# The last two units' input projections made together, with seven products of halves

## The chip, the cores and the metric

One Trainium2 chip, one of its cores. The metric is the device time of one execution of the kernel in microseconds (us): the median of several runs.

## The reference

A linear attention with a decaying state (RWKV-6) is followed by a feed-forward block. All data is fp32.

```python
# r, k, v, w: (4 batches, 8 heads, 768 tokens, 48);  u: (8, 48)
for t in range(S):
    cur = u * k_t (outer) v_t
    y[t] = r_t @ (state + cur)
    state = w_t * state + k_t (outer) v_t
x = y as (3072 tokens, 384)
h = x @ w_in                    # w_in: (384, 2048)
g = h * erf(softplus(h))
out = g @ w_out                 # w_out: (2048, 384)
```

## The kernel before

**Units.** The work is cut into 12 units (n_steps), numbered 0 to 11. A unit has 128 tokens of each of two batches, so 256 tokens (UNIT). A unit goes through three parts: its attention step, which leaves xTs[s], the unit's tokens transposed (384 inner dimensions as KT = 3 blocks of 128 partitions, by 256 tokens); its input projection (hidden); its output projection (project, or project_fast from unit 3 on). The three parts of neighbouring units are interleaved: while step s runs its attention, TensorE is given pieces of the input projection of unit s-1 and of the output projection of unit s-3.

**Input projection.** The 2048 hidden dimensions are 16 blocks of 128, in two groups of FG = 8 (g = 0 and 1). hidden makes two blocks per piece: six products of 128x128 weights by 128x256 tokens (L1027) into one PSUM tile m, of which there are two; ScalarE copies it into the SBUF tile h (L1036). Two pieces make one chunk of 128x1024.

**Activation.** For each chunk ScalarE does softplus into room[:, 0] (softplus_chunk, L983) and erf into the PSUM of y or of pp1 (erf_chunk, L987), and VectorE multiplies h by it in place (multiply_chunk, L992). Softplus and erf need different function tables, so a table load stands before each.

**Output projection.** project_fast does the product of h and w_out as seven products of halves instead of eight. blend makes sums and differences of quarters of h on VectorE (L1112 to L1118, four instructions of 128x1024); mix_weights did the same for w_out once. It yields seven times; each of the seven pieces is eight products of 192 columns (L1135), with copies and adds into o (L1141 to L1167) and the output's DMA.

**Order.** It is written out by hand. From step 5 on, attend_late runs a step and calls run at seven places ("front", "near", 0 to 4); each place has a string of tokens in LATE or USUAL, which run_late executes in order: s, e and m are softplus, erf and multiplication of the next chunk; H is a piece of the input projection of unit s-1; P a piece of the output projection of unit s-3; S the blend of unit s-2; k and F other helpers. After the last step the strings stand in the code: the rest of the attention of unit 11 (from_own L584, fence L593, through_state L610, with the six DMAs of L645 that complete xTs[11]), then

```python
run_late(s, "s P")                      # s = 12, between the two from_own
run_late(s, "m ey m P s P P ep m P P P S H H s H ey m H H s H ep m H H")
run_late(s + 1, "s P ey m P s P P ep m P P P S")
run_late(s + 2, "P P P P P P P")
```

Each engine's instructions stay in the order in which they are emitted, and engines wait for each other through semaphores.

**Names in what follows.** level_products (L552) and take_level work out the attention within a block; state_part (L659) and the adds into middle (L736) carry the state to the second half of the tokens; kT (L718) is an operand of state_part; scale is L328. pp0 and pp1 are two PSUM tiles (products), y another, of the same size, and m two of half that size. words, rest, in, w, rk1, h and o are rotating SBUF tiles.

Of the kernel before, what the change touches and what calls it, by code (L numbers as in the profile page):

```python
# [11 lines left out]
FP32 = mybir.dt.float32  # L12
I32 = mybir.dt.int32
U32 = mybir.dt.uint32
AF = mybir.ActivationFunctionType
ALU = mybir.AluOpType

P = 128
# [5 lines left out]
FG = 8  # L24
FT = 2
# [36 lines left out]
def kernel(  # L62
# [14 lines left out]
    nc = tc.nc  # L77
    PSUM = bass.MemoryType.PSUM

    n_steps, _, _, JP, C = rkw.shape  # L80
    NH, D = v.shape[2:]
    NP = JP // NJ
    NE = NH // JP
    NB, n_pairs = out.shape[:2]
    _, NT, DM = w_out.shape
    KT = DM // P
    UNIT = NJ * C
    NG = NT // FG
# [5 lines left out]
    ins = ctx.enter_context(tc.tile_pool(name="ins", bufs=2))  # L94
    att = ctx.enter_context(tc.tile_pool(name="att", bufs=2))
    xs = ctx.enter_context(tc.tile_pool(name="xs", bufs=2))
    hid = ctx.enter_context(tc.tile_pool(name="hid", bufs=4))
# [33 lines left out]
    def products(shape, n=None):  # L131


        if n is not None:
            return ps_p.tile(shape, FP32, name=f"pp{n}")
        n = turns["next"]
        turns["next"] = 1 - n
        return ps_p.tile(shape, FP32, name=f"pp{n}")
# [934 lines left out]
    def mix_weights():  # L1073

        upper, lower = w_out_sb[:, :FG], w_out_sb[:, FG:]
        b11, b12, b21, b22 = (x[:, :, k * ND : (k + 1) * ND] for x in (upper, lower) for k in range(2))
        t3, t2, t4 = (mixed[:, n] for n in range(3))
        for of, a, op, b in (
            (t3, b22, ALU.subtract, b12), (t2, t3, ALU.add, b11),
            (t4, b21, ALU.subtract, t2), (b12, b12, ALU.subtract, b11),  # L1080
        ):
            engine = yield
            engine.tensor_tensor(out=of, in0=a, in1=b, op=op)
        yield

    blends, lanes = {}, {}

    def quarter(of, what):
# [8 lines left out]
    def blend(of, *parts):  # L1097

        if of not in blends:
            if of < n_steps - 1:  # L1100
                tiles = [room[:, n] for n in (1, 2, 3)]
            else:
                two = att.tile([P, 2, JP, C], FP32, name="rk1", bufs=1)
                one = ins.tile([P, JP, C], FP32, name="w")
                tiles = [x.rearrange("p n t -> p (n t)") for x in (two[:, 0], two[:, 1], one[:])]
            s1, s2, s4 = (x.rearrange("p (f t) -> p f t", t=C) for x in tiles)
            blends[of] = s1, s2, quarter(of, "21"), s4
        s1, s2, s3, s4 = blends[of]
        a = {what: quarter(of, what) if what not in lanes else lanes[what] for what in ("11", "12", "22")}
        for part in parts or (1, 2, 4, 3):  # L1110
            if part == 1:
                nc.vector.tensor_add(s1, s3, a["22"])  # L1112
            elif part == 2:
                nc.vector.tensor_sub(s2, s1, a["11"])
            elif part == 3:
                nc.vector.tensor_sub(s3, a["11"], s3)
            else:
                nc.vector.tensor_sub(s4, a["12"], s2)  # L1118

    def project_fast(s, gs):  # L1120
# [47 lines left out]
                nc.sync.dma_start(out=out[i * NJ, c, :, part], in_=o[0][:, part])  # L1168
        yield

    xTs, hids, projs = {}, {}, {}
    gated = [[] for _ in range(n_steps)]

# [18 lines left out]
    def piece(kind, of):  # L1192
        if not 0 <= of < n_steps:
            return
        if of not in kind:
            if kind is hids:
                kind[of] = hidden(of, xTs[of], gated[of], not of)
            else:
                kind[of] = (project_fast if of >= FAST else project)(of, gated[of])
        next(kind[of])  # L1200

    def in_order(s, k):
# [3 lines left out]
        for what in order[k]:  # L1206
# [12 lines left out]
            "S2 S3 H k12y S4 H F", "s H ep m H H F G s H H H ep",  # L1219
        ),  # L1220
        n_steps - 1: (
            "s P", "m", "ey P m s P P ep P", "m P P", "S", "H H", "s H ey m H H s H ep H H"
        ),
    }
    USUAL = (
# [4 lines left out]
    def run_late(s, tokens, following=None):  # L1230

        for what in tokens.split():
            if what == "A":
                advance()
            elif what == "P":
                piece(projs, s - 3)
            elif what == "H":
                piece(hids, s - 1)
            elif what == "F":
                next(following, None)  # L1240
            elif what == "G":
                mixing.send(nc.gpsimd)
            elif what == "s":
                softplus_chunk()
            elif what[0] == "e":
                erf_chunk(what[1])
            elif what == "m":
                multiply_chunk()
            elif what[0] == "k":
                to_lane(s - 2, what[1:3], what[3])  # L1250
            else:
                blend(s - 2, *(int(n) for n in what[1:]))
                if what == "S3":
                    del lanes["11"], lanes["22"]
                elif what == "S4":
                    del lanes["12"]
# [10 lines left out]
    }  # L1267
    ALONE = {1, 2}

    mixing = mix_weights()  # L1270
    next(mixing)
    make_identity(nc, ident[:])
# [10 lines left out]
    with tc.manual_schedule(  # L1283
        engines={getattr(mybir.EngineType, x) for x in ("PE", "DVE", "Activation", "Pool", "SP")}
    ):
        stay_warm(6)
        for t in (*states[0], *states[1], middle):
            nc.gpsimd.memset(t[:], 0.0)
        nc.gpsimd.memset(over_blocks[:], 1.0)
        nc.scalar.copy(u_row[:, :1], ident[:, :1])  # L1290
        stages, send = convert(
            [
                (into[:, f : f + 2, :], given[:, f : f + 2, :])
                for into, given in ((w_in_sb, w_in), (w_out_sb, w_out))
                for f in range(0, NT, 2)
            ]
        )
        stages["l"](0, loaded[0][0][:, 1, JP - 1, C - 1 : C])
        for s in range(n_steps):
            xTs[s] = xs.tile([P, KT, UNIT], FP32, name="xT")  # L1300
            places = iter(range(8))

            def convert_at(n, late=True):
                if s < len(CONVERT) and n < len(CONVERT[s]):
                    send(CONVERT[s][n][late])

            def place(n):
                if n == LOG - 1 and DIRECT - 1 <= s <= DIRECT:
                    load_rows(s + 2)
                for due in {(3, 4): (5,), (4, 3): (6,), (4, 5): (7,)}.get((s, n), ()):  # L1310
                    load_w(due)
                if s >= DIRECT:
                    in_order(s, next(places))
                    return
                if s in ALONE:
                    if s == 2 and not n:

                        next(hids[0])
                        turns.pop("ahead")()
                    convert_at(n)  # L1320
                    if (s, n) == (1, LOG - 1):
                        load_w(3)
                        load_v(2)
                    if (s, n) == (2, LOG - 2):
                        load_v(3)
                        nc.sync.dma_start(out=block_sb[:], in_=block_mask)
                        nc.sync.dma_start(out=u_row[:], in_=u_rows)
                    if s == 2 and not n:
                        beside(s, next(places))
                        advance(STAGES[s][n])  # L1330
                        return
                    advance(STAGES[s][n])
                else:
                    advance(STAGES[s][n])
                    convert_at(n)
                    if s == DIRECT - 1 and not n:
                        load_rows(DIRECT)
                beside(s, next(places))

            def run(n, following):  # L1340
                if n == 3 and s < n_steps - 2:
                    load_rows(s + 2)
                if n == 3 and s + 3 < n_steps:
                    load_w(s + 3)
                run_late(s, LATE.get(s, USUAL)[STAGES_LATE.index(n)], following)

            if s > DIRECT:
                attend_late(s, run)
                continue
            if s:  # L1350
                attend(
                    s, xTs[s], lambda n: convert_at(n, False), place, lambda: convert_at(LOG + 2)
                )
            else:
                attend_first(xTs[s])
            if s and s + 2 < n_steps:
                load_step(s + 2)
        s = n_steps
        from_own(s - 1, ready[s - 1][0], 1)
        fence()  # L1360
        run_late(s, "s P")
        from_own(s - 1, ready[s - 1][0], 0)
        through_state(s - 1, xTs[s - 1])
        run_late(s, "m ey m P s P P ep m P P P S H H s H ey m H H s H ep m H H")
        run_late(s + 1, "s P ey m P s P P ep m P P P S")
        run_late(s + 2, "P P P P P P P")


# [94 lines left out]
```

## Time and profile before

| | us |
|---|---|
| median of 3 runs | 588.79 |
| lowest and highest | 587.59, 589.34 |
| the profiled execution, its own time | 591.17 |
| its span, first to last instruction | 589.3 |
| TensorE busy | 582.3 (99%) |
| VectorE busy | 434.6 (74%) |
| ScalarE busy | 361.2 (61%) |
| GpSimd busy | 273.4 (46%) |

The span is the time between the first and last instruction of the profiled execution; what lies around it (1.9 us) is in the execution's own time. The mean granted TensorE clock was 0.994. Busy TensorE time is modelled at the ends of matmuls; the chain of waits, which follows the last instruction back to whatever released it, says better where the time goes. A page's row gives line, engine, operation, output and inputs, number, busy time, mean time of one, and the idle time before.

### The profile page before, as it was taken

How to read it: one execution, taken by the hardware profiler on the slowest of the kernel's cores; microseconds unless marked ns; L12 is line 12 of the kernel's file. 1: busy time of each engine (PE TensorE's matmuls, PEld its weight loads, DVE VectorE, ACT ScalarE, POOL GpSimd, SP SyncE). 2: the span in 40 equal slices, each digit the busy share in tenths (PEclk: the TensorE clock that was granted, in tenths of full speed). 3: DMA queues.
4: the chain of work that ended last, by engine and by line, in shares of the span. 5: the costliest groups of instructions: out<-in, count | busy, mean ns of one | idle time of the engine just before them, and what ended most of it. 6: DMA issues, size and time to landing. Idle time of an engine off the chain costs nothing.

```text
span 589.3 us, 16635 instructions
## 1 busy us (share of the span) xinstructions
PE 582.3 (99%) x7256; PEld 500.6 (85%) x7256; DVE 434.6 (74%) x523; ACT 361.2 (61%) x474; POOL 273.4 (46%) x313
## 2 busy tenths in 40 slices
PE   8899999999999999999999999999999999999997
PEld 6688887688668768998998998998898898898997
DVE  6775886899996899799799799799799525023140
ACT  3567878644544598756766766766766754746720
POOL 4557381702398479569369369369359000000000
PEclk9899999999999999999999999999999999999999
DMA  7577572440432514234334334333331300000000
GB/s 258 185 258 292 187 238 61 172 153 10 143 110 103 135 45 160 46 133 153 65 128 159 65 128 150 73 125 116 73 121 42 73 21 14 3 19 15 1 27 28
DMA packets 54081, 63.24 MB, mean 107 GB/s; under 512 B 35160, under 2 KB 40568, under 8 KB 52984
## 3 DMA queue, kind: packets, MB, share of 16 engines
q1 hardware_dynamic: 53624, 61.98, 33.2%
q8 instruction: 57, 0.93, 0.7%
q10 hardware_dynamic: 384, 0.20, 0.1%
q14 instruction: 16, 0.13, 0.1%
HBM read 52.39 MB, written 8.69 MB: 104 GB/s over the span
## 4 chain that ended last, share of the span: by engine, by line
PE 89%; DVE 8%; issue 1%; DMA 1%; POOL 0%; SPq 0%; DVEq 0%; POOLq 0%
PE m L1027 40%; PE m L1135 28%; PE m L1059 6%; PE pp L552 6%; PE y L584 2%; PE pp L659 2%; PE y L610 2%; DVE in L328 2%; PE m L862 1%; DVE words L467 1%; DVE rk L463 1%; DMA rest<-in_w_rows 1%; DVE sums L453 1%; PE pp L871 1%; DVE h L1016 1%
## 5 line engine op out<-in xcount | busy, mean ns | idle before, releaser
L1027 PE MATMUL m<-xT,w_in_sb 128*128 128x256 f32 x1152 | 256.8, 382 | 0.0
L1027 PEld LDWEIGHTS m<-xT,w_in_sb 128*128 128x128 f32 x1152 | 216.4, 190 | 30.5 <-ACT h L1036 0.3
L1036 ACT COPY h<-m 128x512 f32<-128x512 f32 x96 | 55.5, 578 | 83.1 <-PE m L1027 83.1
L328 DVE TENSOR_TENSOR in<-in,tot_sb 128x1024 f32<-128x1024 f32 (+1 forms) x55 | 74.6, 1357 | 15.9 <-PE pp L552 13.7
L463 POOL TENSOR_TENSOR rk<-words 128x528 f32<-128x528 f32 (+3 forms) x28 | 42.4, 1515 | 91.2 <-DVE sums L453 80.8
L467 POOL TENSOR_TENSOR words<-words,rest 128x528 f32<-128x528 f32 (+10 forms) x77 | 78.1, 1015 | 6.0
L1059 PE MATMUL m<-w_out_sb,h 128*128 128x384 f32 x192 | 64.3, 491 | 0.0
L1059 PEld LDWEIGHTS m<-w_out_sb,h 128*128 128x128 f32 x192 | 35.7, 190 | 23.5
L1135 PE MATMUL m<-mixed,h 128*128 128x192 f32 x288 | 51.1, 331 | 0.0
L983 ACT ACT_TABLE_LOAD x36 | 46.2, 1283 | 2.8 <-issue 2.1
L1135 PE MATMUL m<-w_out_sb,h 128*128 128x192 f32 x272 | 47.5, 329 | 0.0
L1135 PEld LDWEIGHTS m<-mixed,h 128*128 128x128 f32 x288 | 46.6, 190 | 0.9
L987 ACT ACT_TABLE_LOAD x36 | 46.2, 1283 | 1.6 <-DVE room L1118 1.1
L1135 PEld LDWEIGHTS m<-w_out_sb,h 128*128 128x128 f32 x272 | 44.3, 190 | 0.4
L1135 PE MATMUL m<-w_out_sb,room 128*128 128x192 f32 x256 | 44.2, 326 | 0.0
L552 PEld LDWEIGHTS pp<-in 48*64 48x64 f32 (+1 forms) x2368 | 33.4, 126 | 11.6 <-issue 6.0
L1135 PEld LDWEIGHTS m<-w_out_sb,room 128*128 128x128 f32 x256 | 42.0, 190 | 0.0
L992 DVE TENSOR_TENSOR h<-h,y 128x1024 f32<-128x1024 f32 x17 | 20.7, 1216 | 28.3 <-ACT y L987 28.1
L402 POOL TENSOR_TENSOR tot_sb<-tot_sb 128x256 f32<-128x256 f32 (+4 forms) x50 | 37.1, 742 | 3.8
L983 ACT ACTIVATE room<-h 128x1024 f32<-128x1024 f32 x36 | 38.1, 1057 | 0.4
L992 DVE TENSOR_TENSOR h<-h,pp 128x1024 f32<-128x1024 f32 x19 | 23.1, 1213 | 19.5 <-ACT pp L987 19.5
L552 PE MATMUL pp<-in 48*64 48x32 f32 (+1 forms) x2368 | 37.1, 212 | 0.2 <-DVE in L328 0.2
(147 smaller groups left out, 830.5 us busy)
## 6 DMA issues: line engine op xcount, KB each, us to landing
in<-in_rkw SPq DMA_DIRECT2D x8, 1024.0 KB, 5.7
words<-in_moe_w_in SPq DMA_DIRECT2D x16, 384.0 KB, 6.1
words<-in_moe_w_out SPq DMA_DIRECT2D x16, 384.0 KB, 5.8
words<-in_rk_rows SPq DMA_DIRECT2D x8, 768.0 KB, 6.4
w<-in_rkw SPq DMA_DIRECT2D x11, 512.0 KB
v<-in_v SPq DMA_DIRECT2D x12, 384.0 KB, 5.7
out<-o SPq DMA_DIRECT2D x23, 192.0 KB, 2.9
in<-in_rkw SPq DMA_DIRECT2D x7, 512.0 KB, 5.8
```

The source lines that it names most:

```text
L328: nc.vector.tensor_mul(halves, halves, view(tots[level - 1], 0, [[1, n], [2, nb], [0, half]]))
L402: nc.gpsimd.tensor_mul(new, pair[:, :, 0], pair[:, :, 1])
L463: engine.tensor_mul(terms[n], r[:, :, n:], k[:, :, : near - n])
L467: engine.tensor_mul(k[:, :, :m], k[:, :, :m], w[:, :, n : n + m])
L552: nc.tensor.matmul(to, lhsT=rk(1, n)[rows(e), s0 : s0 + m], rhs=right, start=True, stop=True,)
L983: nc.scalar.activation(sp_room, chunks[0], AF.Softplus)
L987: nc.scalar.activation(at, sp_room, AF.Erf)
L992: nc.vector.tensor_mul(h, h, at)
L1027: nc.tensor.matmul(ps[:, ff, :], lhsT=w_in_sb[:, g * FG + f + ff, kk * P : (kk + 1) * P], rhs=xT[:, kk, :], start=kk == 0, stop=kk == KT - 1,)
L1036: nc.scalar.copy(h[:, f : f + FT, :], ps[:])
L1059: nc.tensor.matmul(ps[j][:], lhsT=gs[g][:, f, j * C : (j + 1) * C], rhs=w_out_sb[:, g * FG + f, :], start=g + f == 0, stop=g == NG - 1 and ...
L1135: nc.tensor.matmul(to, lhsT=a[:, f], rhs=b[:, f], start=start and f == 0, stop=f == FG - 1, skip_group_check=True,)
```

## The change

The input projections of units 10 and 11 are no longer made one after the other, but together, at the very end. Written with the two groups of hidden blocks as rows, and the inner dimension's first two blocks of 128 as columns, w_in is a matrix of two by two; the tokens of the two units are the other factor, of two by two as well (inner block by unit). Seven products of such halves take the place of eight, with sums of weights (join_weights, s1 to s4, once) and differences of tokens (join_tokens, t1 to t4). The third inner block is added by plain products; where one plain product can serve two results, the difference of the two units' third blocks is used (less).

hidden_of_two yields seven times (J1 to J7 here) for each pair of blocks of both groups, four pairs in all. Its accumulators are m0, a half of y, low, a half of pp0, and high, a half of pp1; each holds 128x512. Results are copied by ScalarE or VectorE into h11, h21 (unit 10) and h12, h22 (unit 11), and later parts are added there by VectorE. The activation goes by chunks of 512 with new tokens: u is softplus, v is erf in place, z the multiplication. The last two chunks, of 1024, are done by s, e and m as before. The H, and the S, of the last step's places are taken out. Q is a P of one unit later; w one instruction of join_weights.

```diff
+    def half_room(name, shape):
+        t = wide.tile(shape, I32, name=name, bufs=3 if name == "words" else 2)
...
     def blend(of, *parts):
         if of not in blends:
-            if of < n_steps - 1:
+            if of < n_steps - 2:
                 tiles = [room[:, n] for n in (1, 2, 3)]
+            elif of == n_steps - 1:
+                tiles = [half_room("words", [P, 2, DM, 2])[:, : FG * C] for _ in range(3)]
             else:
                 two = att.tile([P, 2, JP, C], FP32, name="rk1", bufs=1)
...
+    def third(g, kk):
+        return w_in_sb[:, g * FG : (g + 1) * FG, kk * P : (kk + 1) * P]
+
+    def join_weights():
...
+        a11, a12, a21, a22 = (third(g, kk) for g in range(NG) for kk in range(2))
+        turns["joint weights"] = s1, s2, a21, s4
+        for out_, a, op, b in (
+            (s1, a21, ALU.add, a22), (s2, s1, ALU.subtract, a11),
+            (s4, a12, ALU.subtract, s2), (a21, a11, ALU.subtract, a21),
+        ):
+            nc.vector.tensor_tensor(out=out_, in0=a, in1=b, op=op)
+            yield
+
+    def join_tokens():
...
+        one, two = ([xTs[of][:, kk, :] for kk in range(KT)] for of in (n_steps - 2, n_steps - 1))
+        for out_, a, b in (
+            (t1, two[0], one[0]), (t2, two[1], t1), (t4, one[1], t2), (less, one[2], two[2]),
+            (t3, two[1], two[0]),
+        ):
+            nc.vector.tensor_sub(out_, a, b)
...
+    def hidden_of_two():
...
+        m0 = y[:, :, 0].rearrange("p e j t -> p e (j t)")
+        low, high = (products([P, NE, 2, UNIT], n)[:, :, 0] for n in range(2))
+        s1, s2, s3, s4 = turns["joint weights"]
+        x, z, t1, t2, t3, t4, less = turns["joint tokens"]
+        a11, a12, up, _, a22, down = (third(g, kk) for g in range(NG) for kk in range(KT))
+
+        def add_up(to, start, *factors):
+            for k, (a, b) in enumerate(factors):
+                for e in range(NE):
+                    nc.tensor.matmul(
+                        to[:, e], lhsT=a[:, 2 * i + e], rhs=b,
+                        start=start and not k, stop=True, skip_group_check=True,
+                    )
+
+        pairs = FG // 2
+        for i in range(pairs):
+            f = slice(2 * i, 2 * i + 2)
+            add_up(m0, True, (a11, x[0]))
+            nc.scalar.copy(h11[:, f], m0)
+            yield
+            add_up(low, True, (a12, x[1]), (up, x[2]))
+            nc.vector.tensor_add(h11[:, f], h11[:, f], low)
+            chunks.append(h11[:, f])
+            yield
+            add_up(high, True, (s1, t1))
+            nc.scalar.copy(h22[:, f], high)
+            yield
+            add_up(m0, False, (s2, t2))
+            nc.vector.tensor_copy(h12[:, f], m0)
+            yield
+            add_up(low, True, (a22, t4), (down, less))
+            nc.scalar.copy(h21[:, f], low)
+            yield
+            add_up(m0, False, (s3, t3), (down, z[2]))
+            nc.vector.tensor_add(h21[:, f], h21[:, f], m0)
+            nc.vector.tensor_add(h22[:, f], h22[:, f], m0)
+            chunks.append(h21[:, f])
...
+            yield
+            add_up(high, False, (s4, z[1]), (up, z[2]))
+            nc.vector.tensor_add(h12[:, f], h12[:, f], high)
...
+    def activate_pair(what):
+        if what == "u":
...
+            nc.scalar.activation(at, h, AF.Softplus)
...
+        elif what == "v":
+            h, at = slots["u"].pop(0)
+            nc.scalar.activation(at, at, AF.Erf)
...
+        else:
+            h, at = slots["v"].pop(0)
+            nc.vector.tensor_mul(h, h, at)
...
         n_steps - 1: (
-            "s P", "m", "ey P m s P P ep P", "m P P", "S", "H H", "s H ey m H H s H ep H H"
+            "s P", "m w", "ey P m s P P ep P", "m P P", "", "", ""
         ),
...
         s = n_steps
         from_own(s - 1, ready[s - 1][0], 1)
         fence()
-        run_late(s, "s P")
+        run_late(s - 1, "S Q w w w")
         from_own(s - 1, ready[s - 1][0], 0)
         through_state(s - 1, xTs[s - 1])
-        run_late(s, "m ey m P s P P ep m P P P S H H s H ey m H H s H ep m H H")
-        run_late(s + 1, "s P ey m P s P P ep m P P P S")
+        run_late(s, "P P P P T")
+        run_late(s, "J J J J J u J u u J")
+        run_late(s, "J u v J J v J z z J v v J z u u u J z")
+        run_late(s, "J u v J J v J z z J v v J z u u J z")
+        run_late(s, "J J u v J J z v J z v J z u v J z P P S s ey")
+        run_late(s + 1, "P P m s ep P P m P P P S")
         run_late(s + 2, "P P P P P P P")
```

T stands for join_tokens and the start of hidden_of_two, J for its next yield.

More of the change, by code (lines that the diff above doesn't have):

```diff
@@ L1084, in mix_weights @@
         yield
+    def half_room(name, shape):
+        t = wide.tile(shape, I32, name=name, bufs=3 if name == "words" else 2)
+        t = t[:].rearrange("p a b two -> p (a b two)" if len(shape) == 4 else "p a b -> p (a b)")
+        return t.bitcast(FP32)
     blends, lanes = {}, {}
@@ L1169, in project_fast @@
         yield
+    def third(g, kk):
+        return w_in_sb[:, g * FG : (g + 1) * FG, kk * P : (kk + 1) * P]
+    def join_weights():
+        s1, s2, s4 = (
+            half_room("words", [P, 2, DM, 2])[:, : FG * P].rearrange("p (f m) -> p f m", m=P)
+            for _ in range(3)
+        )
[7 more added lines that the diff above has]
+            yield
@@ new lines, in join_tokens @@
+    def join_tokens():
+        made = ins.tile([P, 2, JP, C], FP32, name="in")
+        made = made[:].rearrange("p x n t -> p (x n t)").rearrange("p (i t) -> p i t", t=UNIT)
+        t1, t2, t3, t4, less = (made[:, i] for i in range(5))
+        one, two = ([xTs[of][:, kk, :] for kk in range(KT)] for of in (n_steps - 2, n_steps - 1))
[4 more added lines that the diff above has]
+            nc.vector.tensor_sub(out_, a, b)
+        turns["joint tokens"] = one, two, t1, t2, t3, t4, less
@@ new lines, in hidden_of_two @@
+    def hidden_of_two():
+        one, two = n_steps - 2, n_steps - 1
+        h11, h21 = (hid.tile([P, FG, UNIT], FP32, name="h")[:] for _ in range(NG))
+        h12 = room[:, 2:4].rearrange("p i n -> p (i n)").rearrange("p (f t) -> p f t", t=UNIT)
+        h22 = ins.tile([P, 2, JP, C], FP32, name="in")
+        h22 = h22[:].rearrange("p x n t -> p (x n t)").rearrange("p (f t) -> p f t", t=UNIT)
+        gated[one].extend((h11, h21))
+        gated[two].extend((h12, h22))
+        m0 = y[:, :, 0].rearrange("p e j t -> p e (j t)")
[9 more added lines that the diff above has]
+                        start=start and not k, stop=True, skip_group_check=True,
+                    )
+        pairs = FG // 2
[21 more added lines that the diff above has]
+            chunks.append(h21[:, f])
+            if i < pairs - 2:
+                chunks.append(h22[:, f])
+            yield
+            add_up(high, False, (s4, z[1]), (up, z[2]))
+            nc.vector.tensor_add(h12[:, f], h12[:, f], high)
+            if i < pairs - 2:
+                chunks.append(h12[:, f])
+            elif i == pairs - 1:
+                chunks.extend(h[:, 2 * i - 2 : 2 * i + 2] for h in (h12, h22))
+            yield
@@ new lines @@
+    slots = {"next": 0, "u": [], "v": []}
+    def activate_pair(what):
+        if what == "u":
+            h = chunks.pop(0)
+            i, k = divmod(slots["next"] % 4, 2)
+            slots["next"] += 1
+            n = FT * UNIT
+            at = room[:, i, k * n : (k + 1) * n].rearrange("p (f t) -> p f t", t=UNIT)
+            nc.scalar.activation(at, h, AF.Softplus)
+            slots["u"].append((h, at))
+        elif what == "v":
+            h, at = slots["u"].pop(0)
+            nc.scalar.activation(at, at, AF.Erf)
+            slots["v"].append((h, at))
+        else:
+            h, at = slots["v"].pop(0)
+            nc.vector.tensor_mul(h, h, at)
@@ L1240, in run_late @@
                 next(following, None)
+            elif what == "Q":
+                piece(projs, s - 2)
+            elif what == "J":
+                next(turns["joint"])
+            elif what == "w":
+                next(joining)
+            elif what in "uvz":
+                activate_pair(what)
+            elif what == "T":
+                join_tokens()
+                turns["joint"] = hidden_of_two()
             elif what == "G":
@@ L1268 @@
     ALONE = {1, 2}
+    joining = join_weights()
     mixing = mix_weights()
```

## The prediction

> **What bounds the kernel now.** I read the busy times of the page first, then the chain of waits from 440 us to the end, then the timelines of ScalarE (ACT) and VectorE (DVE) over the same stretch.
>
> ```profile
> PE 582.3 (99%) x7256; PEld 500.6 (85%) x7256; DVE 434.6 (74%) x523; ACT 361.2 (61%) x474; POOL 273.4 (46%) x313
> ```
>
> TensorE (PE) is busy 99% of the span. That is an average, so the stage that is edited must be looked at by itself. This is its chain of waits (start, length, what):
>
> ```profile
> 486.72 0.85 PE pp L659 x32
> 487.57 20.92 PE m L1027 x96
> 508.49 0.59 PE y L584 x32
> 509.08 2.80 PE m L1135 x16
> 511.88 0.59 PE y L584 x32
> 512.47 0.90 PE y L610 x64
> 513.37 15.80 PE m L1135 x96
> 529.17 20.72 PE m L1027 x96
> 549.88 33.80 PE m L1135 x208
> 583.69 2.61 PE pp L1135 x16
> 586.30 0.02 issue
> 586.32 0.35 DVE o L1167
> ```
>
> From 487.57 to 586.30 us there is nothing but TensorE work, end to end: no wait for another engine. The two L1027 rows are the input projections of units 10 and 11 (48 products each; each fp32 product has two MATMUL records, hence x96), L1135 the output projections, L584 and L610 the end of the last attention step. So time is saved by having fewer products, as long as the others keep TensorE fed. Their prices, one row per form:
>
> ```profile
> 495.84 0.57 ACT L1036 COPY h<-m 128x512 f32<-128x512 f32 x1
> 496.43 1.28 ACT L987 ACT_TABLE_LOAD   x1
> 497.72 1.03 ACT L987 ACTIVATE y<-room 128x1024 f32<-128x1024 f32 x1
> 498.69 0.58 ACT L1036 COPY h<-m 128x512 f32<-128x512 f32 x1
> 498.79 1.22 DVE L992 TENSOR_TENSOR h<-h,y 128x1024 f32<-128x1024 f32 x1 [5.66 <-ACT y L987]
> ```
>
> The copy takes 0.58, a change of function 1.28 and the next activation follows within 0.01, a 1024-wide activation about 1.04. These rows also say something on waits: the copy at 498.69 and the multiplication at 498.79 work on other slices of one h tile at once, though the multiplication is earlier in program order. Waits follow the slices, not whole tiles, and I use that below.
>
> **The Trainium skill.** (1) "FP8 and Floating Point Precision", TensorE Precision Notes: a true FP32 product takes four passes of the array. The trace agrees: 20.92/48 = 0.436 us for 256 columns, and the 192-column product takes 2.60/8 = 0.325, the same time per column. (2) "ScalarE: Activation LUTs", What ACT_TABLE_LOAD costs: 1283 ns for the load and some 1380 ns of drain, 2.66 us a switch. The trace has the 1283, but not the drain: the activation starts 1.29 after the load began. The measurement decides; the page's figure is the upper bound in a rival. (3) "VectorE: DVE Perf Modes", The TRN2 errata: an fp32 tensor_tensor costs (N+151)/0.96 ns, 691 for N = 512; the trace's 512-wide L328 row took 0.69. (4) "PSUM — Partial Sum Buffer", PSUM bank collisions: two engines must not touch one bank at once. That is why a product that adds into an accumulator must wait until what was there has been copied out; the trace of before shows no such wait that TensorE loses time to.
>
> **The change part by part.**
>
> *Products.* Before, units 10 and 11 need 96 products of 256 columns. After, one pair of blocks has 2+4+2+2+4+4+4 = 22 (the seven yields J1 to J7 of hidden_of_two), four pairs 88. The two rows hold 41.64 us for 96, so 0.434 each: 88 cost 38.17, **3.47 us less**. All of it lies on the chain.
>
> *Cover that goes.* The eight H of unit 10 covered the last attention step from 487.57 to 508.49. Now L584 follows L659 at once. It needs own, whose last copies on ScalarE ended at 482.5: ready. Q (2.60) ends at about 490.8, L584 again until 491.4, then L610 to 492.3. L610 needs middle. The two L736 adds (0.55 each) stood behind the four blends on DVE; S is now emitted later, so they run at 487.6 to 488.8: ready 2.6 us early. The fence (0.17) follows. The four P cover 492.3 to 502.7.
>
> *S moved.* The four blends of unit 9 (1.23 each, DVE) run from 489.0 to 494.0; s1 is wanted by the third piece at 494.9 and is there at 490.3.
>
> *Weights, tokens.* Four DVE instructions of 1024 elements, 1.22 each. The first comes ahead of the kT multiplication (L718, 468.7) and delays it to about 470; its reader L659 runs at 486.7. The other three run to 497.7. For the tokens, L610's end at 492.3 is followed by the y3 and xT copies (1.2) and six DMAs on SP's queue: in the trace issuing them took 4.10 and each landed after 1.8, so the last is there at about 499.2. Five 256-wide subtractions at about 0.4 (between the 0.35 of 192 and 0.55 of 384 columns) end at 501.2. J3, their first reader, starts at 505.3: hidden with 4 us to spare. J1 and J2 use unit 10's own tokens.
>
> *Emptying the accumulators.* 16 ScalarE copies become 12, and 20 DVE instructions of 512 elements (0.69) are new. Each has to be over before its accumulator is written again: m0 after J1, a copy of 0.60 under J2+J3 (2.6 us); low after J2, an add under J3+J4 (1.74); m0 after J4, a copy under J5 (1.74); high after J3, a copy under J4 to J6 (4.3); **m0 after J6, two adds, 1.38 and two handovers of about 0.1, under J7 (1.74)**; high after J7, an add under the next J1+J2 (2.6). The tightest keeps 0.2 us. DVE has 9 x 0.69 = 6.2 us of work in a pair of 9.54.
>
> *Activations.* 12 chunks of 512 by u and v, two of 1024 by s and e. A 512-wide activation is not in the trace. Bounds: the copy's 0.58 below, three quarters of the 1024-wide row, 0.78, above; I take 0.60 (the copies of 1024 and 512 differ by 0.44; 1.04 less that). ScalarE in the second pair: 3 copies 1.8, four u and four v 4.8, two loads 2.6, **9.2 of 9.54**; the first pair has 4.9, the third 8.6, the fourth, with three loads, 9.3. It is therefore the engine that sets the order here. Walking the queues from 502.7, the copies come late by 1 to 2 us, but always inside the room above; the last v ends at about 544.0, its z at 544.8. J ends at 541.0 and the two P of unit 9 run to 546.2, and only then does unit 10's first piece want that z: 1.4 to spare.
>
> *End.* Blends of unit 10 start at 546.8, s1 is there at 548.1 and wanted at 551.4. The first copy into o waits for unit 9's out DMA (issued about 546.9, landing in 1.9): perhaps 0.3 for ScalarE, where the last s and e queue; their m is wanted at 564. The last blends stand as before. TensorE's waits on semaphores in J (28 places instead of 16) I take at nothing: the P of before carry such waits and run at the bare 0.325 a product. If each new one cost 0.05, it would be 0.6; below nothing has no reason.
>
> Sum: -3.47. The profiled execution took 591.17 us with a span of 589.3; I expect about 585.8 for the span. The median of the runs shown is 2.4 lower than the profiled execution; the same step from it gives 588.79 - 3.5 = **585.3**.
>
> **Rivals.** A difference under 0.3% (1.8 us) can't be told from none here.
>
> *Gaps in J.* With handovers of 0.3 instead of 0.1 and activations at 0.70, m0 comes 0.36 late at the start of three pairs, and unit 10's first piece waits 1.7: 2.7 us back, 588.0. For: 0.2 us and 1.4 us are thin. Against: the handovers seen are short (erf's end at 498.75, multiplication at 498.79).
>
> *ScalarE becomes the bound, slower.* The place is J2 of the second pair to the first piece of unit 10, the price the load: seven loads lie there. With the drain of the page, 7 x 1.38 = 9.7 late, less the 1.4 of room: 8.3, and 4.8 net, about 593.6. The gain is gone from (3.5+1.4)/7 = 0.7 us per load on. For: ScalarE is filled to 96%. Against: the trace shows 1.29.
>
> *The attention's end is exposed.* If the tokens came over 4 us later than worked out, J3 would wait for them. Four more us would return the gain: 588.8. Against: six DMAs at 0.68 are in the trace.
>
> That the number of products isn't what is said can be excluded from the loops.
>
> **How the numbers follow.** Forecast 0.76: 585.3, with its own range from 584.3 (scatter of the runs, 0.7, and 0.3 for the estimate) to 587.0. Gaps and late tokens together 0.14, around 588. ScalarE the bound 0.10, around 593.6. The range, 584.3 to 588.0, takes in the forecast and about half of the gaps. Faster by over 0.3%: 0.77; within: 0.13; slower: 0.10.
>
> **What would show it.** Right: 176 records of the joint products in about 38.2 us with no idle time before them but tenths; the chain still all TensorE, ending near 582.9; the last v on ScalarE near 544; table loads at 1.28. Wrong: TensorE waiting for a copy or add in J (the gaps), or for h ahead of unit 10's first L1135 (ScalarE), or J3 waiting for the token subtractions. A span above 588 would refute the sum.

## The result, and the profile after

Six runs of the changed kernel had a median of 585.62 us (584.44 to 586.88), six of the kernel before 588.26; the ratio is 0.9954, 95% interval 0.9937 to 0.9971: 2.6 us less, between 1.7 and 3.7. Timed again on another occasion it had 584.80 (first experiment). The prediction was 585.3.

The page's busy times have 16 MATMUL records fewer than before, eight products:

```profile
PE 576.4 (99%) x7240; PEld 495.1 (85%) x7240; DVE 454.7 (78%) x558; ACT 355.6 (61%) x478; POOL 274.1 (47%) x313
```

The chain of waits of the changed kernel over the stretch that was shown of before (start, length, what). L1142 is now the line of the output projection's products, L1230 that of the joint ones, L1174 the last add into o:

```profile
486.25 0.81 PE pp L659 x30
...
487.10 0.45 PE y L584 x30
487.55 2.80 PE m L1142 x16
490.35 0.59 PE y L584 x32
490.94 0.90 PE y L610 x64
491.84 10.60 PE m L1142 x64
502.44 0.86 PE y L1230 x4
503.30 2.59 PE pp L1230 x12
...
538.70 1.73 PE pp L1230 x8
540.42 39.00 PE m L1142 x240
579.42 2.61 PE pp L1142 x16
582.04 0.02 issue
582.06 0.35 DVE o L1174
```

It is still TensorE alone, end to end. L584 follows L659 with nothing between, where 96 records stood before, and the joint products lie where the input projection of unit 11 ended. From the start of L659 to the last add it is 582.06 - 486.25 = **95.81 us, against 586.32 - 486.72 = 99.60 before: 3.79 less**. I use this length, the tail, to compare profiles below, because everything ahead of it is the same in all kernels but for one VectorE instruction. In the tail the granted clock is 1.00 in both; the mean of 0.994 in the profile of before comes from 25 to 50 us, where it was 0.87 (see the last section).

The windows of busy time say the same for the joint stretch alone (TensorE, weight loads, VectorE, ScalarE, GpSimd, each with its instructions, then granted clock, DMA share and GB/s):

```profile
502.27:540.26 37.99, 37.99 (x178) 33.24 (x177) 18.89 (x30) 27.93 (x42) 0.00 (x0) 1.00 0.00 1
```

TensorE is filled. ScalarE is busy for 27.9 of 38.0 us, so it is not the bound, though it is close in parts.

### The profile page after: what moved, and what is told of

Read it like the earlier page. It is cut to its first block, busy times and chain, and to the rows that moved or that the text cites. A ratio compares the mean times of both kernels' runs of the same rounds, so it can differ in the third digit from the quotient of the medians.

```text
span 585.1 us, 16663 instructions
## 1 busy us (share of the span) xinstructions
PE 576.4 (99%) x7240; PEld 495.1 (85%) x7240; DVE 454.7 (78%) x558; ACT 355.6 (61%) x478; POOL 274.1 (47%) x313
## 4 chain that ended last, share of the span: by engine, by line
PE 95%; DVE 3%; issue 1%; ACT 0%; POOL 0%; DVEq 0%; POOLq 0%
PE m L1027 36%; PE m L1142 28%; PE m L1059 8%; PE pp L552 6%; PE pp L1230 4%; PE y L1230 2%; PE y L584 2%; PE pp L659 2%; PE y L610 2%; PE m L862 1%; PE pp L871 1%; PE pp L938 1%; DVE in L328 1%; DVE words L467 1%; PE pp L1142 0%
## 5 line engine op out<-in xcount | busy, mean ns | idle before, releaser
L1027 PE MATMUL m<-xT,w_in_sb 128*128 128x256 f32 x960 | 215.3, 382 | 0.1
L1027 PEld LDWEIGHTS m<-xT,w_in_sb 128*128 128x128 f32 x960 | 179.9, 190 | 26.2 <-issue 1.0
L1036 ACT COPY h<-m 128x512 f32<-128x512 f32 x80 | 46.4, 579 | 57.6 <-PE m L1027 57.5
L1142 PE MATMUL m<-mixed,h 128*128 128x192 f32 x256 | 45.6, 331 | 0.0
L1142 PE MATMUL m<-w_out_sb,h 128*128 128x192 f32 x256 | 44.8, 329 | 0.0
L1142 PEld LDWEIGHTS m<-mixed,h 128*128 128x128 f32 x256 | 41.4, 190 | 0.9
L1142 PEld LDWEIGHTS m<-w_out_sb,h 128*128 128x128 f32 x256 | 41.6, 190 | 0.3
L1142 PE MATMUL m<-w_out_sb,room 128*128 128x192 f32 x240 | 41.5, 326 | 0.0
L1142 PEld LDWEIGHTS m<-w_out_sb,room 128*128 128x128 f32 x240 | 39.4, 190 | 0.0
L463 POOL TENSOR_TENSOR words<-words 128x336 f32<-128x336 f32 (+6 forms) x49 | 35.3, 720 | 3.8
L453 DVE TENSOR_REDUCE sums<-rk 128x14 f32<-128x672 f32 (+9 forms) x54 | 34.7, 701 | 0.0
L453 DVE TENSOR_REDUCE sums<-words 128x6 f32<-128x288 f32 (+8 forms) x66 | 26.9, 464 | 3.9 <-POOL words L463 3.6
```

The lines of the kernel that those rows point to most:

```text
L453: nc.vector.tensor_reduce(out=view(sums[:], n, [[near * (NEAR + 1), NEAR // near], [NEAR + 1, near - n]]), in_=terms[n], axis=mybir.AxisLi ...
L463: engine.tensor_mul(terms[n], r[:, :, n:], k[:, :, : near - n])
L1027: nc.tensor.matmul(ps[:, ff, :], lhsT=w_in_sb[:, g * FG + f + ff, kk * P : (kk + 1) * P], rhs=xT[:, kk, :], start=kk == 0, stop=kk == KT - 1,)
L1036: nc.scalar.copy(h[:, f : f + FT, :], ps[:])
L1142: nc.tensor.matmul(to, lhsT=a[:, f], rhs=b[:, f], start=start and f == 0, stop=f == FG - 1, skip_group_check=True,)
```

## The experiments

### The change timed again

No edit.

> The changed kernel unaltered, timed in more rounds. Theory (fewer products, TensorE without gaps): the two traces differ by 3.8 us from L659 on, so 3.5 to 3.8 us less than before, ratio 0.9936 to 0.9941. Rival (part of the 3.8 us is lost where one profile doesn't show it, since the medians differ by 2.6 only): 2.6 us or less, ratio 0.9955 or more.

584.80 us (583.70 to 587.62), ratio to before 0.9936, interval 0.9912 to 0.9961: 3.8 us. The profile's tail is 483.35 to 579.16, again 95.81 to the hundredth. The rival expected 0.9955 or more, which this interval does not quite exclude. The tails speak for 3.8; the medians of single occasions scatter more than that difference. Most of it arises in the first 100 us, here in the windows of the changed kernel's two profiles, the first one above:

```profile
0.00:100.00 100.00, 94.93 (x1996) 75.08 (x1996) 71.61 (x90) 67.29 (x115) 54.18 (x70) 1.00 0.63 211
0.00:100.00 100.00, 95.72 (x2064) 75.90 (x2065) 74.16 (x93) 68.47 (x117) 53.20 (x71) 1.00 0.65 218
```

One program, and 68 TensorE records more in the same time: L659 was reached at 486.25 in one and at 483.35 in the other. What makes the start vary I did not try.

### Eight products put back

```diff
             add_up(m0, True, (a11, x[0]))
+            add_up(m0, True, (a11, x[0]))
```

> Each J1 is issued twice (the second overwrites the first): 8 products more, 96 as before, all else of the change in place. Theory (the gain is the number of products alone): 8 x 0.432 = 3.45 us above the changed kernel, equal to the kernel before within 0.4 us. Rival (the new order, the removed cover or the new emptying brings or costs something of its own): it differs from the kernel before by more than 1 us.

588.30 us, ratio to before 0.9991 (0.9978 to 1.0005); tail 484.62 to 583.88 = 99.26 us, 3.45 over the changed kernel and 0.34 under the kernel before. Everything else of the change is in this kernel: the uncovered attention, the new emptying, the regrouped activations. They cost nothing that can be measured. (The second J1 also gives each pair 0.86 us more in which to empty its accumulators; that the changed kernel does without is seen from its chain, which has no wait.) The gain is the eight products, at 3.45/8 = 0.431 us each, and a remainder of 0.34, for which see the sum below.

### m0 set free later

```diff
             nc.vector.tensor_add(h21[:, f], h21[:, f], m0)
+            for _ in range(2):
+                nc.vector.tensor_copy(spare, m0)
             nc.vector.tensor_add(h22[:, f], h22[:, f], m0)
```

> Between the two adds after J6 VectorE copies m0 twice to a spare tile: m0 comes free 1.2 to 1.4 us later. Theory (the two adds fit under J7 with 0.2 us or less to spare): TensorE waits 0.9 to 1.15 us at the start of pairs two, three and four, 2.6 to 3.5 us in all over the changed kernel, with the last pair and the rest unmoved. Rival (there is a microsecond of room, the handover is not tight): under 1 us in all.

589.37 us, ratio to before 1.0010 (0.9992 to 1.0027): the gain is gone. Tail 99.74, 3.93 over the changed kernel. From its waits (total, times, longest) and its TensorE timeline:

```profile
PE y L1230 <- DVE in L1260: 3.1, 3, 1.0
```

```profile
510.27 1.13 PE L1230 MATMUL y<-xT,w_in_sb 128*128 128x256 f32 x4 [1.04 <-DVE in L1260]
```

Three waits of 1.04, where the theory had 0.9 to 1.15. The two copies moved the second add by 1.32 (1.41 of busy time, overlapping its neighbours), so the room in the changed kernel was 1.32 - 1.04 = 0.28 us. But 3.93 is more than 3.1, and more than the 3.5 at most that was expected: the chain has 1.13 for the first four records after each wait, where it has 0.86 elsewhere, so each restart costs 0.27 besides.

### Softplus and erf alternating

```diff
-        run_late(s, "J u v J J v J z z J v v J z u u u J z")
+        run_late(s, "J u v J J J z z J J z u v u v u v J z")
```

and the other three J strings in the same way.

> Every u is followed at once by its v, so softplus and erf alternate: 24 table loads in J instead of 8. Theory (ScalarE keeps up only because the functions are grouped, and has about 1.9 us of room): 16 x 1.29 = 20.6 us more on ScalarE, less the room: 18 to 19 us over the changed kernel, with TensorE waiting for ScalarE's copy of h11 at J4 of the later pairs. Rival (ScalarE has much room, or a load can be hidden in its waits for TensorE): under 8 us.

604.02 us, ratio to before 1.0260 (1.0225 to 1.0294), so 19.2 us over the changed kernel's 584.80. The profile, which was the longest of the four executions, has a tail of 117.02, 21.2 over. Its waits, and windows after the first of them and well after the last:

```profile
PE y L1230 <- ACT h L1239: 13.5, 3, 5.9
```

```profile
521.00:527.00 6.00, 6.00 (x15) 4.76 (x16) 2.42 (x4) 4.72 (x7) 0.00 (x0) 0.52 0.01 1
...
562.00:580.00 18.00, 18.00 (x113) 18.00 (x112) 8.95 (x10) 11.29 (x13) 0.00 (x0) 1.00 0.06 23
```

TensorE waits for ScalarE's copy of h11 behind the table loads, as the theory said, and only the grouping of u and v keeps this away. What it did not expect is the 0.52 in the first line: after the wait of 5.9 us the granted clock is half for about 6 us. So the agreement with the 18 to 19 expected is partly luck. Those were to be waits alone, but the waits are 13.5 (5.9, 5.6 and 2.0); the other 7.7 of the 21.2 lies nearly all in products at half the clock. The added loads cost less waiting than worked out; ScalarE was idle for some 10 us of J in the changed kernel, which leaves more room than the 1.9 taken, but where the loads went I did not follow up. The rival's 8 us is refuted.

### Tokens made later

```diff
+        for _ in range(8):
+            nc.vector.tensor_add(spare, s1, s2)
         for out_, a, b in (
             (t1, two[0], one[0]), (t2, two[1], t1), (t4, one[1], t2), (less, one[2], two[2]),
```

> Eight VectorE additions of 1024 elements, into a spare tile, stand ahead of the five token subtractions: the tokens come 8 x 1.22 = 9.8 us later. Theory (the tokens were ready 5.9 us before J3, so the removed cover costs nothing): t1 is there at about 507 by the changed kernel's clock, J3 waits 2.0 to 2.5 us, and 2.2 to 3.0 us are lost in all. Rival (the tokens or what follows them on VectorE were already close to the limit): 6 us or more.

588.30 us, ratio to before 1.0000 (0.9984 to 1.0016); tail 484.48 to 584.43 = 99.95, 4.14 over the changed kernel. TensorE timeline, then windows:

```profile
505.57 2.08 PE L1235 MATMUL pp<-in,words 128*128 128x256 f32 x4 [2.30 <-DVE in L1212]
507.44 1.69 PE L1235 MATMUL y<-in,words 128*128 128x256 f32 x4
508.96 1.89 PE L1235 MATMUL pp<-in,w_in_sb 128*128 128x256 f32 x8
```

```profile
505.50:506.50 1.00, 0.93 (x2) 0.84 (x3) 0.88 (x4) 0.00 (x0) 0.00 (x0) 0.50 0.00 0
...
508.50:509.50 1.00, 1.00 (x5) 0.83 (x5) 0.34 (x1) 0.00 (x0) 0.00 (x0) 0.87 0.00 0
```

The wait is 2.30, inside the 2.0 to 2.5 expected. Counted from L659, t1 was ready 9.97 later than in the changed kernel, so J3's room there was 9.97 - 2.30 = 7.7; the 5.9 of the expectation is the room of the last token difference, which J3 does not read. The loss of 4.14 was outside what I had, 2.2 to 3.0. After 2.3 us without work the clock is 0.50 for some 3 us, and the eight records of J3 and J4 take 3.5 us instead of 1.7.

### ScalarE given more work

One softplus of 1024 elements (x) in the last J string, then three. Only the first diff is shown; x is nc.scalar.activation from part of w_in_sb into a spare tile.

```diff
-        run_late(s, "J J u v J J z v J z v J z u v J z P P S s ey")
+        run_late(s, "J J u v J J z v J z v J z u x v J z P P S s ey")
```

> One softplus of 1024 elements into a spare tile is added on ScalarE after the twelfth u, 1.0 us. Theory (the last z is 1.9 us ahead of the first output piece of unit 10): no TensorE wait, no change. Rival (ScalarE sets the end of this stretch already): the first piece of unit 10 comes 1 us later.

One run, 585.36 us; tail 95.81, no TensorE wait. The added microsecond is hidden.

> Three such softplus, 3.0 to 3.1 us more on ScalarE at the same place. Theory (1.9 us of room): TensorE waits 1.1 to 1.2 us ahead of unit 10's first output piece, 1.2 to 1.5 us lost in all. Rival (no room): 3 us lost; rival (the work is hidden by later waits of ScalarE): nothing lost.

586.37 us, ratio to before 0.9961 (0.9951 to 0.9972); tail 97.62, 1.81 over the changed kernel, where I had 1.2 to 1.5. Waits, and two rows of VectorE's timeline:

```profile
PE m L1142 <- DVE o L1162: 1.5, 1, 1.5
```

```profile
544.83 0.69 DVE L1287 TENSOR_TENSOR h<-h,room 128x512 f32<-128x512 f32 x1 [4.66 <-ACT room L1283]
545.44 0.55 DVE L1162 TENSOR_TENSOR o<-o,m 128x384 f32<-128x384 f32 x1
```

The wait of unit 10's first piece names L1162, not the z (L1287). L1162 is unit 9's add into o, which reads one m tile and so sets it free; that piece wants this tile. It has nothing to do with ScalarE, but it stands behind the late z in VectorE's queue and ends 0.55 after it. That takes 0.5 from the room of 1.9 that I had read off the z, and leaves 1.4; by the experiment it was 1.6, as L1162 came 3.12 later and TensorE waited 1.54. The remaining 1.81 - 1.54 = 0.27 is the same price of starting again as in the m0 experiment.

## Why the prediction was right

**The sum.** The step was 3.47, the tails show 3.79. That the median of 585.62 lies so close to the 585.3 is partly luck, as two medians of this kernel lie 0.8 apart; the tails are the better evidence. Two terms are off, both small. The 88 products took 37.98 in the chain (502.44 to 540.42) instead of 38.17: I had spread over all 96 a piece of about 0.2 us that the first row has once, where TensorE goes from 64-wide products to wide ones (20.92 against 20.72 in the rows of before). And L659 with the first L584 takes 1.30 (486.25 to 487.55) instead of 0.85 + 0.59 = 1.44, as L584 now overlaps L659's last records. Together they are the 0.3 by which the step was too small. Over 96 products, the first of them is 0.20, and 0.20 + 0.14 is the 0.34 that the kernel with eight products put back is under the kernel before. The sum uses the measured price only: an equal time per column at 256 and at 192 columns fits the four passes in the prediction's first note, but would fit another fixed number too.

**The cover.** Worked as laid out: no wait between L659 and the joint products. This is VectorE's timeline of the changed kernel:

```profile
487.22 1.12 DVE L736 TENSOR_TENSOR middle<-faded,pp 48x384 f32<-48x384 f32 x2 [0.38 <-PE pp L659]
...
496.90 0.41 DVE L1207 TENSOR_TENSOR in<-xT 128x256 f32<-128x256 f32 x1
...
498.21 0.75 DVE L1207 TENSOR_TENSOR in<-xT 128x256 f32<-128x256 f32 x2
```

middle is there at 488.3, the tokens at 499.0, not 501.2: the first subtraction starts as soon as VectorE is done with the weights, 0.3 us after SP issued the last of the six DMAs (492.58 to 496.63), and I had let it wait until all had landed. J3 starts at 504.9, 5.9 after the last of the five, not 4. But I had counted to the wrong one: J3 reads t1 alone, which is ready at 497.3 and has 7.6 us to spare, while the last, t3, is wanted only by J6.

**The accumulators.** The two adds after J6 end at 511.60 in the first pair and m0 is written again from 511.77:

```profile
510.31 0.69 DVE L1255 TENSOR_TENSOR h<-h,y 128x512 f32<-128x512 f32 x1 [2.83 <-PE y L1230]
510.92 0.68 DVE L1256 TENSOR_TENSOR in<-in,y 128x512 f32<-128x512 f32 x1
```

The predicted 0.2 of room was 0.28 by experiment. The wait needs no rule on PSUM banks, which the prediction gave as its reason: a product written into m0 too early would change what is still to be read. No run here tells the two reasons apart. The bound for TensorE's waits on semaphores, nothing to 0.6, came out at nothing.

**ScalarE.** This is the last part of its timeline in J:

```profile
534.34 0.63 ACT L1279 ACTIVATE room<-h 128x512 f32<-128x512 f32 x1 [1.93 <-DVE h L1242]
534.99 1.28 ACT L1283 ACT_TABLE_LOAD   x1
536.29 0.63 ACT L1283 ACTIVATE room<-room 128x512 f32<-128x512 f32 x1
...
542.18 0.63 ACT L1283 ACTIVATE room<-room 128x512 f32<-128x512 f32 x1
```

The 512-wide activation took 0.63, or 0.53 when the next one overlaps it; 0.60 was taken. The last v ended at 542.8, where about 544 was expected. A switch costs 1.28 and the activation follows within 0.02, so the drain that the Trainium skill adds ("ScalarE: Activation LUTs", What ACT_TABLE_LOAD costs) is not there, and with it goes the slower rival's price. Its mechanism was sound: with 16 loads more TensorE waited for ScalarE for 13.5 us.

**Where the working failed without being punished.** First, the 1.4 us to spare ahead of unit 10 was counted to the z of h21. The z leaves 1.9; the right limit is the L1162 behind it, which I had not counted, and it happens to leave 1.4 as well (1.6 by the experiment): luck. What is queued behind a late instruction was the question, and I asked it for ScalarE only. Second, the rival of gaps was priced at the length of the waits. A gap costs more: 0.27 each for 1.0 or 1.5 us, 1.8 for 2.3 us. Third, the cover of the tokens was counted to an operand that J3 does not read; the conclusion held because the true room was larger.

## What to carry to other kernels

Where one engine is filled end to end, the price of an edit is that engine's own work, and the rest of the working consists in showing for each new wait which work covers it and how much is left over; here the smallest remainder was 0.28 us, and two small VectorE copies in each pair turned the gain of 3.8 us into nothing. Follow a late instruction through its whole queue, since whoever waits for the next one there waits too. Compare profiles over the stretch that the edit touches, from one common instruction to the end: that was the same to the hundredth where whole runs differed by 3 us.

## What was unexpected of the hardware

A gap in TensorE's work costs more than its length. After waits of 1.04 and 1.54 us the granted clock stayed 1.00 and the restart cost 0.27 us; after 2.30 us it was 0.50 for some 3 us and the restart cost 1.8; after 5.9 us it was half for about 6 us. The third wait of the alternating kernel was shorter than 2.30 and cost as much. Here is its row of TensorE's timeline, then the windows that follow it:

```profile
553.21 1.27 PE L1230 MATMUL y<-in,words 128*128 128x256 f32 x4 [2.01 <-ACT h L1239]
```

```profile
553.21:554.07 0.86, 0.86 (x4) 0.78 (x5) 0.67 (x1) 0.86 (x1) 0.00 (x0) 1.00 0.00 0
554.07:557.48 3.41, 3.41 (x10) 2.67 (x9) 1.89 (x3) 3.37 (x5) 0.00 (x0) 0.50 0.00 0
```

TensorE had worked again for 0.86 us at the full clock when it was halved, and J4 and J5 took 4.55 us there instead of 2.59. The half clock lasted 3.41 us here and after the wait of 2.30, and 6.83, twice that, after the waits of 5.9 and 5.6. In this kernel it began at 519.93, 537.00 and 554.07, each time 17.07 later, five times 3.41. So in these traces the clock seems to change in steps of about 3.41 us rather than when a gap begins or ends; that is an estimate from these four spells and the one that follows.

The Trainium skill ("TensorE: Matmul & The Clock Gate", Why this matters for your kernels) warns of gaps over about 3 us; here 2.0 and 2.3 were enough, in the one profile of each. Nor is the length all: in the profile of before the clock was halved for 6.83 us from 24.75 on, in a stretch of products of 48 and 64 columns whose longest gap was 1.24, while the gap of 1.54 among wide products left it alone. What decides, the work done in a step or where the gap lies in it, no experiment here tells.
